# Second layers one turn later, odd tiles through the DMA transpose, and a condition around the last two half slots

## The chip, the core and the metric

The kernel runs on one core of a Trainium2 chip. The metric is the device time of one execution in microseconds, lower is better. Times of several runs are given by their median.

## What is computed

Three stages, on x of shape (8, 3072, 256); after the first one the 24576 rows of 256 are tokens:

```python
# 1: a filter in the frequency domain along the sequence
X = np.fft.rfft(x, axis=1)
y = np.fft.irfft(X * F[None], n=3072, axis=1)
# 2: a layer of 1024, then back to 256
h = y @ w_in
e = np.exp(h - h.max(-1)); sm = e / (e.sum(-1) + 1e-9)
solu = h * sm
ln = (solu - mu) / np.sqrt(var + 1e-6) * g_ln
x2 = ln @ w_out
# 3: one of 8 experts for each token, by the largest cosine
logits = normed(x2) @ normed(expert_emb).T / tau
idx = logits.argmax(1); gate_w = softmax(logits)[row, idx]
out[idx == e] = gate_w * (np.maximum(x2 @ w1[e], 0) @ w2[e])
```

## The kernel before

**Precision.** Every large matmul is made of three f16 matmuls (high x high, high x low, low x high), which is why tiles are split into a high and a low half by one ACT copy and one DVE subtraction.

**Stage B** (`stage_b`) goes over 192 tiles of 128 tokens, 48 for each of four pairs of batches. Turn i of its loop issues, in program order: the transposes of tile i-1 (`turn`) if it has any; the exponential of tile i on ACT (L929) and its product on DVE (L930), which make `es`; in even turns the inverse transform of two more tiles (`inv4`, L710 to L716); the second layer of tile j = i - LAG (L945, 24 matmuls into `o`); work from other generators (`aux`); the first layer of tile i+1 (`begin`, `mm1`, L728, 12 matmuls of 512 columns into the PSUM tile `h`) and its row maximum (`top`, L893). Engines keep program order, so the order of these calls is the order on every queue. `h` has two buffers; a tile that is turned keeps its buffer until T is out, as its transposes are written into it.

The second layer needs `es` transposed, as f16 halves, in `T`. There are two ways to it. `turn` (L899) makes eight f32 transposes on PE into `h`, an ACT copy (L907) and a DVE subtraction (L908). `send` (L910) makes the ACT copy (L914) and the subtraction (L915) first, from `es` into `hl`, and one DMA from SP's queue (L917) transposes the result into `T`. In the first three pairs even tiles are turned at the start of the next turn and odd tiles are sent at the end of their own turn, behind the second layer; in the last pair every tile is turned.

`aux` gives out side work: in pairs 0 to 2 the Fourier transforms of the next pair (`fft`) and the maxima of the expert weights (`w_max`); in the last pair, from turn LAG of it, the split of the expert weights into `wexp` (`w_split`, L452 and L460), done by turn SPLIT. Every eight second layers a group is closed by `b_final`, which runs over the next turns, chooses experts and places, and scatters the tokens' numbers into lists. `early` (`first_slots`), one step per turn at the end, makes the first table of slots.

**Stage C** (`stage_c`) goes over 110 slots: 89 of 256 tokens, then 21 half slots of 128. A slot is one expert's block of tokens: `load_slot` gathers the rows (POOL, L1121) and transposes them by DMA (SP, L1126), `weights` copies the expert's weights (DVE, L1149), then comes the first layer (L1197), its split (L1200, L1201), the second layer (L1160, for half slots one slot later), a scaling on ACT (L1163) and a scatter into the output on POOL (`scatter`, L164). The tables (`table`, `other_slots`) say which expert and tokens a slot has; 21 half slots are the most that any routing can need, and a slot that is not needed gathers an empty row and its scatter writes nothing. `run` opens the pools: `bx` for the tiles of pairs 0 to 2, `bp` for those of the last.

Of the kernel before, what the change touches and what calls it, by code (L numbers as in the profile page):

```python
# [32 lines left out]
EARLY = 24  # L33
LAG = 2
FIRST = 2
UNITS = 24 + 8 + 64 + 4
READY = 42
SPLIT = 38
WAIT = 4
MAGIC = 0x5F3759DF  # L40

# [111 lines left out]
class Build:  # L153
# [703 lines left out]
    def stage_b(self, xp, bps, gp, ps, hp, op, aux, early):  # L857
# [63 lines left out]
        for i in range(n + LAG):  # L921
            j = i - LAG
            now = 0 <= i < n
            if 0 <= i - 1 < n and i != n - 1 and (i % 2 or i > n - N2):
                turn(i - 1)
            if now:
# [22 lines left out]
            if now:  # L949
                if i % 2 and i < n - N2:  # L950
                    send(i)
                aux(*divmod(i, N2), 0)
                if i + 1 < n:
                    begin(i + 1)
                    top(i + 1)
                jk = L["pool"].tile([128, FF], BF16, name="jk", tag="jk")
                nc.scalar.activation(jk, L["s"], AF.Square, accum_out=col(i, "st", 2))
# [8 lines left out]
            if 0 <= j < n:  # L966
# [13 lines left out]
                if k == G - 1:  # L980
                    p, nn = divmod(j - (G - 1), N2)
                    finals.append((self.b_final(groups.pop(j // G), p, nn, gp, ps, j // G == n // G - 4, j // G < n // G - 4), 0))
            if i >= n - N2 + SPLIT + 2:
                next(early, 0)
# [23 lines left out]
    def table(self, sp, tp, ps, nb, start, K, blk, out):  # L1008
# [19 lines left out]
        v.scalar_tensor_tensor(taken, taken, 0.0, nb, op0=ALU.max, op1=ALU.min)  # L1028
        out["taken"] = taken
        yield  # L1030
        ge = sp.tile([128, E], F32, name="ge", tag="ge")
# [63 lines left out]
    def other_slots(self, sp, tp, ps):  # L1095
# [15 lines left out]
        yield  # L1111
        yield from self.table(sp, tp, ps, nb, x2, rest, 128, {})

# [15 lines left out]
    def stage_c(self, cb, hp, op, ps, side):  # L1129

        nc = self.nc
        wt = {}

        def load(s):
            while s >= len(self.tables):
                if next(side, 1) == 1:
                    return
            for _ in self.load_slot(s, cb):
                pass
# [12 lines left out]
        def second(M):  # L1152

            tab, k, w2, hh, hl, fs = M
            for h in range(tab["nh"]):
# [10 lines left out]
                next(side, 0)  # L1166

        weights(0, 0)
        next(side)
        load(1)  # L1170
        weights(0, 1)
        s = 0
        late = None
        while s in self.loaded:
            load(s + 2)
            xT = self.loaded.pop(s)
            tab, k = self.tables[s]
            w1, w2 = wt[s]
            n = tab["nh"] * 128
            w1 = w1.rearrange("p (l k f) -> p l k f", l=2, k=2)  # L1180
            w2 = w2.rearrange("p (l k f) -> p l k f", l=2, k=8)
            m = 512 // n
            fs = 1024 // n
            hh, hl = [], []
            for j in range(8 // m):
                if j == 8 // m - 2:
                    weights(s + 1, 0)
                if m * j % fs == 0:
                    hh.append(cb.tile([128, fs, n], F16, name="chh", tag="chh", bufs=2))
                    hl.append(cb.tile([128, fs, n], F16, name="chl", tag="chl", bufs=2))  # L1190
                t = (ps.tile([128, m, n], F32, name="a", tag="a") if j % 2 else hp.tile([128, m, n], F32, name="h", tag="h"))
                for i in range(m):
                    f = m * j + i
                    q = 0
                    for db in range(2):
                        for l, r in ((0, 0), (1, 0), (0, 2)):
                            nc.tensor.matmul(t[:, i, :], w1[:, l, db, f * 128:(f + 1) * 128], xT[:, r + db, :n], start=q == 0, stop=q == 5)  # L1197
                            q += 1
                sl = slice(m * j % fs, m * j % fs + m)
                nc.scalar.activation(hh[-1][:, sl, :], t, AF.Relu)  # L1200
                nc.vector.scalar_tensor_tensor(hl[-1][:, sl, :], t, 0.0, hh[-1][:, sl, :], op0=ALU.max, op1=ALU.subtract)  # L1201
                next(side, 0)
            if late:
                second(late)
            weights(s + 1, 1)
            late = (tab, k, w2, hh, hl, fs)
            if tab["nh"] > 1:
                second(late)
                late = None
            wt.pop(s)  # L1210
            s += 1
        if late:
            second(late)


    def run(self):
        tc, nc = self.tc, self.nc
        last = self.np_run - 1
        with (
# [14 lines left out]
            bps = [None, None]  # L1234
            bps[0] = right.enter_context(Tags(tc, "bx", {"nm": 2, "es": 2, "jk": 1, "hl": 2, "T": 3}, side="right"))
            ap = right.enter_context(tc.tile_pool(name="ap", bufs=2, side="right"))
            with (
# [3 lines left out]
                with tc.tile_pool(name="pp", bufs=1) as pp:  # L1241
# [5 lines left out]
                    for pool, tag in ((xp, "c4"), (xp, "xh"), (gp, "rows")):  # L1247
                        self.m1 += [pool.tile([128, 4, 128], F32, name=tag, tag=tag, bufs=2) for _ in range(2)]
                    self.m1 += [pp.tile([128, 4, 128], F32, name=f"m1_{k}") for k in range(2)]
                    for _ in self.fft(0, ap, ps, hp):  # L1250
# [14 lines left out]
                def last_pool():  # L1265
                    for _ in ffts:
                        pass
                    mid.close()
                    bps[1] = mid.enter_context(Tags(tc, "bp", {"nm": 2, "es": 2, "jk": 1, "T": 3}))

# [83 lines left out]
```

## Time and profile before

| | before |
|---|---|
| median of 3 runs | 2769.92 us (2764.28 to 2777.8) |
| the profiled execution | 2770.33 us |
| its span, first to last instruction | 2768.5 us |
| mean granted clock of TensorE | 0.983 |
| PE, DVE, ACT, POOL busy | 2642.6, 1897.8, 1529.8, 1245.2 us |

The span is what the profile covers; the execution's own time lies 1.8 us above it. Times in rows are microseconds from the span's start. PE is TensorE's matmuls, PEld its weight loads, DVE VectorE, ACT ScalarE, POOL GpSimd, SP SyncE; a q behind a name is that engine's sequencer. Busy times are unions, so two overlapping instructions count once. The releaser of a wait, behind an arrow, is inferred from semaphores.

### The profile page before, as it was taken

To read this page: it belongs to the slowest core of one execution; us is meant where nothing else is said; L and a number is where in the kernel's file an instruction comes from. 1 tells how busy PE (TensorE), PEld (TensorE's weight loads), DVE (VectorE), ACT (ScalarE), POOL (GpSimd) and SP (SyncE) were. 2 spreads that over 40 slices of the span, in tenths; PEclk is the share of its full clock that TensorE was granted. 3 is DMA by queue.
4 is the path that set the end of the run, shared out by engine and by line. 5 is a ranking of instruction groups with operands and counts; after the bars stand their busy time and mean duration, and the time that the engine had idled before them with its cause. 6 is when DMAs were issued, how large, how long until landed. Compare 5 with 4: busy or idle time off the path is not lost.

```text
span 2768.5 us, 53941 instructions
## 1 busy us (share of the span) xinstructions
PE 2642.6 (95%) x20234; PEld 2035.6 (74%) x20234; DVE 1897.8 (69%) x2976; ACT 1529.8 (55%) x2858; POOL 1245.2 (45%) x2633
## 2 busy tenths in 40 slices
PE   6889999999999998999999998999999999999998
PEld 5447666666666675666677777888888888888898
DVE  5846888867898768988788985554544545545465
ACT  3556777767777766877788864323333333333332
POOL 2001245434555444554455556744454444544444
PEclk8999999999999999999999999999999999999999
DMA  9868888799787798876444432332222333223222
GB/s 316 221 178 248 196 209 185 186 218 211 178 196 181 204 231 201 187 172 140 104 123 121 120 72 50 78 77 73 77 77 75 78 75 78 76 75 79 75 59 57
DMA packets 445398, 384.66 MB, mean 139 GB/s; under 512 B 285995, under 2 KB 368053, under 8 KB 442064
## 3 DMA queue, kind: packets, MB, share of 16 engines
q1 hardware_dynamic: 392288, 310.60, 46.6%
q0 software_dynamic: 27088, 57.48, 6.8%
q10 hardware_dynamic: 25760, 13.14, 1.8%
q8 instruction: 159, 2.61, 0.4%
q14 instruction: 103, 0.84, 0.1%
HBM read 195.93 MB, written 103.35 MB: 108 GB/s over the span
## 4 chain that ended last, share of the span: by engine, by line
PE 30%; issue 23%; POOL 19%; DVE 14%; DMA 8%; ACT 4%; SPq 1%; POOLq 0%; ACTq 0%; DVEq 0%
PE h L728 10%; PE o L945 9%; POOL crow L1121 7%; POOL out_dram L164 6%; POOL scr L163 3%; DVE nm L893 3%; DVE es L930 2%; PE a L512 2%; PE h L904 2%; PE a L667 2%; PE a L710 2%; DMA bufA<-out 2%; DMA c<-bufC 1%; DVE T L908 1%; ACT hl L914 1%
## 5 line engine op out<-in xcount | busy, mean ns | idle before, releaser
L945 PE MATMUL o<-wo_h,T 128*128 128x264 f16 x3072 | 552.8, 277 | 3.3 <-DMA T<-hl 3.2
L1160 PE MATMUL o<-cw,chh 128*128 128x256 f16 x3184 | 527.6, 273 | 0.0
L728 PE MATMUL h<-win_h,xh 128*128 128x512 f16 x1536 | 497.3, 385 | 25.8 <-DVE T L908 22.5
L1197 PEld LDWEIGHTS <-cw 128*128 128x128 f16 x5280 | 476.1, 98 | 57.3 <-POOL gu L761 6.5
L945 PEld LDWEIGHTS <-T 128*128 128x128 f16 x4608 | 452.4, 98 | 70.0 <-DMA T<-hl 3.6
L896 POOL TENSOR_SCALAR gcc<-nm 128x1 f32<-128x1 f32 x192 | 118.6, 618 | 813.3 <-DVE nm L894 533.6
L728 PEld LDWEIGHTS <-xh 128*128 128x128 f16 x2304 | 223.6, 99 | 310.3 <-issue 81.2
L1160 PE MATMUL o<-cw,chl 128*128 128x256 f16 x1592 | 434.0, 273 | 3.0 <-DVE chl L1201 3.0
L945 PE MATMUL o<-wo_l,T 128*128 128x264 f16 x1536 | 425.5, 277 | 0.0
L164 POOL DMA_INDIRECT out_dram<-cot,ids x199 | 218.4, 1097 | 454.8 <-ACT cot L1163 443.0
L1201 DVE SCALAR_TENSOR_TENSOR chl<-h,chh 128x512 f16<-128x512 f32 x199 | 135.8, 683 | 392.1 <-ACT chh L1200 392.1
L1160 PEld LDWEIGHTS <-chh 128*128 128x128 f16 x3184 | 310.6, 98 | 35.5
L1163 ACT ACTIVATE cot<-o,fac 128x256 f32<-128x256 f32 x199 | 94.5, 475 | 423.8 <-PE o L1160 421.8
L1149 DVE COPY cw<-wexp 128x4096 f16 x220 | 279.9, 1280 | 44.3 <-PE o L1160 23.6
L893 DVE TENSOR_REDUCE nm<-h 128x1 f32<-128x1024 f32 x192 | 234.0, 1219 | 105.5 <-PE h L728 105.3
L1197 PE MATMUL h<-cxT,cw 128*128 128x256 f16 (+1 forms) x2640 | 295.1, 263 | 6.8 <-POOL gu L761 6.2
L728 PE MATMUL h<-win_l,xh 128*128 128x512 f16 x768 | 295.9, 385 | 0.0
L1197 PE MATMUL a<-cxT,cw 128*128 128x256 f16 (+1 forms) x2640 | 294.0, 262 | 0.0
L930 DVE SCALAR_TENSOR_TENSOR es<-h,gcc,es 128x1024 f32<-128x1024 f32 x192 | 245.6, 1279 | 65.3 <-ACT es L929 49.4
L929 ACT ACTIVATE es<-h,nm,isc_h 128x1024 f32<-128x1024 f32 x192 | 230.7, 1201 | 61.6 <-DVE nm L894 46.0
L1121 POOL DMA_INDIRECT crow<-xs,ids x199 | 203.5, 1022 | 65.8 <-issue 63.8
L164 POOL DMA_INDIRECT lst<-gdi,gix x192 | 209.1, 1089 | 35.1 <-issue 32.9
(262 smaller groups left out, 4355.9 us busy)
## 6 DMA issues: line engine op xcount, KB each, us to landing
wst<-in_w_dram SPq DMA_DIRECT2D x128, 256.0 KB
in<-in_x_dram SPq DMA_DIRECT2D x48, 512.0 KB
in<-bufA SPq DMA_DIRECT2D x64, 384.0 KB
c<-bufC SPq DMA_DIRECT2D x96, 256.0 KB
xs<-rows SPq DMA_DIRECT2D x96, 256.0 KB
ft<-in_filt_dram SPq DMA_DIRECT2D x24, 960.0 KB
bufA<-out SPq DMA_DIRECT2D x72, 256.0 KB
zw<-z SPq DMA_DIRECT2D x96, 192.0 KB
```

Of the source, the lines that this page charges most:

```text
L164: ins = self.nc.gpsimd.indirect_dma_start(in_offset=None, **kw).ins
L728: nc.tensor.matmul(h[:, nb, :], l[:, i, db, :], r[:, db, sl], start=k == 0, stop=k == 5)
L893: nc.vector.tensor_reduce(x[:, 0:1], L["h"], axis=AX.X, op=ALU.max, negate=True)
L896: nc.gpsimd.tensor_scalar(cc, nm, nm, 1.0, op0=ALU.mult, op1=ALU.max)
L929: nc.scalar.activation(L["s"], L["h"], AF.Exp, bias=L["nm"], scale=self.isc_h[:, i // N2:i // N2 + 1], accum_out=col(i, "st", 0))
L930: nc.vector.scalar_tensor_tensor(L["s"], L["h"], col(i, "cc", 0), L["s"], op0=ALU.mult, op1=ALU.mult, accum_out=col(i, "st", 1))
L945: nc.tensor.matmul(o[:, :D + E], T[:, l, :], r[:, f, :], start=q == 0, stop=q == 23)
L1121: nc.gpsimd.indirect_dma_start(out=rows[:, h, :], out_offset=None, in_=self.xs, in_offset=bass.IndirectOffsetOnAxis(ap=tab["ids"][:, h, k: ...
L1149: nc.vector.tensor_copy(w.rearrange("p (o k) -> p o k", o=1), self.wexp[:, bass.ds(e, 1), part * 4096:(part + 1) * 4096])
L1160: nc.tensor.matmul(o[:, :D], l[f // fs][:, f % fs, h * 128:(h + 1) * 128], w2[:, r, f, :], start=q == 0, stop=q == 23)
L1197: nc.tensor.matmul(t[:, i, :], w1[:, l, db, f * 128:(f + 1) * 128], xT[:, r + db, :n], start=q == 0, stop=q == 5)
L1201: nc.vector.scalar_tensor_tensor(hl[-1][:, sl, :], t, 0.0, hh[-1][:, sl, :], op0=ALU.max, op1=ALU.subtract)
```

## The change

LAG is 3 in place of 2, so the second layer of tile j stands in turn j + 3. Odd tiles are sent at the start of the turn after their own, where even tiles are turned, in all four pairs; tile 191 is still turned. `T` has four buffers, and the last pair's pool has one `hl`. The split of the expert weights and `early` start one turn later. Two of the first matrices move from the pool `pp` to tiles `mt` of `ap`. In stage C the table keeps the count of half slots that hold tokens (`used`); the loop over slots becomes a function, stops two slots early, and runs the last two only if the count is over 19.

```diff
-LAG = 2
+LAG = 3
+SPARE = 2
...
-            if 0 <= i - 1 < n and i != n - 1 and (i % 2 or i > n - N2):
-                turn(i - 1)
+            if 0 <= i - 1 < n and i != n - 1:
+                (turn if i % 2 or i == n else send)(i - 1)
...
             if now:
-                if i % 2 and i < n - N2:
-                    send(i)
                 aux(*divmod(i, N2), 0)
...
-            if i >= n - N2 + SPLIT + 2:
+            if i >= n - N2 + SPLIT + LAG:
                 next(early, 0)
...
         out["taken"] = taken
+        used = out["used"] = tp.tile([1, 1], I32, name=f"used{len(self.tables)}")
+        v.tensor_copy(used, src[0:1, E - 1:E])
...
-        yield from self.table(sp, tp, ps, nb, x2, rest, 128, {})
+        t2 = {}
+        yield from self.table(sp, tp, ps, nb, x2, rest, 128, t2)
+        self.used = t2["used"]
...
+        stop = [None]
         def load(s):
...
+            if stop[0] is not None and s >= stop[0]:
+                return
...
+        def slots(s):
+            late = None
+            while s in self.loaded:
...
+        n = self.np_run * 2 * S
+        full = -(-(n - E * (BLK - 1)) // BLK)
+        rest = (n - full * BLK - E) // 128 + E
+        end = full + rest
+        stop[0] = end - SPARE
         weights(0, 0)
         next(side)
         load(1)
         weights(0, 1)
...
+        slots(0)
+        assert len(self.tables) == end
+        used = nc.values_load(self.used[0:1, 0:1], min_val=0, max_val=end)
+        with tc.If(used > rest - SPARE):
+            stop[0] = end
+            for s in range(end - SPARE, end):
+                load(s)
+            weights(end - SPARE, 0)
+            weights(end - SPARE, 1)
+            slots(end - SPARE)
...
-            bps[0] = right.enter_context(Tags(tc, "bx", {"nm": 2, "es": 2, "jk": 1, "hl": 2, "T": 3}, side="right"))
+            bps[0] = right.enter_context(Tags(tc, "bx", {"nm": 2, "es": 2, "jk": 1, "hl": 2, "T": 4}, side="right"))
...
-                    self.m1 += [pp.tile([128, 4, 128], F32, name=f"m1_{k}") for k in range(2)]
+                    self.m1 += [ap.tile([128, 4, 128], F32, name="mt", tag="mt", bufs=3) for _ in range(2)]
...
-                    bps[1] = mid.enter_context(Tags(tc, "bp", {"nm": 2, "es": 2, "jk": 1, "T": 3}))
+                    bps[1] = mid.enter_context(Tags(tc, "bp", {"nm": 2, "es": 2, "jk": 1, "hl": 1, "T": 4}))
```

## Rows read from the trace of the kernel before

**Rows 1.** Page, part 1: busy us, share of span, instructions.

```profile
PE 2642.6 (95%) x20234; PEld 2035.6 (74%) x20234; DVE 1897.8 (69%) x2976; ACT 1529.8 (55%) x2858; POOL 1245.2 (45%) x2633
```

**Rows 2.** Windows by stage: start:end length, PE, PEld, DVE, ACT, POOL busy, clock, DMA share, GB/s.

```profile
186.00:596.90 410.90, 386.78 (x2406) 262.25 (x2405) 319.02 (x506) 294.68 (x554) 143.94 (x400) 0.98 0.82 200
...
1366.10:1704.00 337.90, 322.58 (x2387) 236.68 (x2386) 281.62 (x544) 252.59 (x485) 183.37 (x539) 0.99 0.39 100
1704.00:2760.50 1056.50, 1049.04 (x10081) 942.99 (x10081) 544.47 (x689) 332.37 (x598) 531.23 (x663) 1.00 0.29 74
```

**Rows 3.** Windows again: a full stretch, eight turns of pair three, eight of the last.

```profile
750.00:800.00 50.00, 48.70 (x322) 32.94 (x320) 47.39 (x78) 41.05 (x77) 29.97 (x66) 1.00 0.78 179
1314.90:1366.10 51.20, 50.26 (x356) 35.23 (x355) 40.35 (x83) 38.27 (x75) 25.21 (x83) 1.00 0.48 103
1474.00:1528.60 54.60, 53.35 (x395) 39.20 (x394) 48.34 (x89) 44.38 (x85) 29.14 (x84) 1.00 0.46 120
```

**Rows 4.** Waits of PE: us, times, longest; 186 to 1366.1, last row 1366.1 to 1700.

```profile
PE h L728 <- DVE T L908: 17.1, 11, 3.7
PE a L710 <- DMA c<-bufC: 6.7, 4, 3.0
...
PE o L945 <- DMA T<-hl: 3.2, 2, 2.8
...
PE h L728 <- DVE T L908: 5.4, 5, 1.3
```

**Rows 5.** Timeline of PE, one even turn of the last pair: start, length, instruction.

```profile
1482.68 0.38 PE L728 MATMUL h<-win_h,xh 128*128 128x512 f16 x1
...
1485.27 1.04 PE L904 MATMUL h<-cst,es 128*128 128x128 f32 x8
1486.14 1.06 PE L710 MATMUL a<-mt,c 128*128 128x128 f32 x8
1489.73 0.38 PE L728 MATMUL h<-win_h,xh 128*128 128x512 f16 x1
```

**Rows 6.** Groups by line, whole span: busy us, mean ns, idle before, releasers.

```profile
L908 DVE TENSOR_TENSOR T<-h,T 128x1024 f16<-128x1024 f32 x120 | 145.1, 1209 | 30.2 <-ACT T L907 29.9
...
L915 DVE TENSOR_TENSOR hl<-es,hl 128x1024 f16<-128x1024 f32 x72 | 88.1, 1223 | 43.3 <-ACT hl L914 43.3
```

**Rows 7.** Timeline of DVE in the same turns; idle before it in brackets.

```profile
1481.41 1.22 DVE L908 TENSOR_TENSOR T<-h,T 128x1024 f16<-128x1024 f32 x1
...
1485.47 1.23 DVE L893 TENSOR_REDUCE nm<-h 128x1 f32<-128x1024 f32 x1 [0.58 <-PE h L728]
```

**Rows 8.** DMA of 1900 to 2600: queue's packets, MB, share; issues.

```profile
q1 hardware_dynamic: 72199, 17.41, 13.2%
...
cxT<-crow SPq DMA_TRANSPOSE x133
```

**Rows 9.** Timeline of DVE in pair three, tiles 127 and 128.

```profile
1245.70 1.22 DVE L915 TENSOR_TENSOR hl<-es,hl 128x1024 f16<-128x1024 f32 x1 [0.73 <-ACT hl L914]
...
1247.97 1.21 DVE L893 TENSOR_REDUCE nm<-h 128x1 f32<-128x1024 f32 x1
```

**Rows 10.** Waits of SP's queue, 200 to 1366: us, times, longest.

```profile
SPq L917 <- DVE hl L915: 329.7, 59, 9.9
```

**Rows 11.** Timeline of PE: the first slot of stage C.

```profile
1703.95 2.72 PE L1197 MATMUL h<-cxT,cw 128*128 128x256 f16 x12 [6.23 <-POOL gu L761]
```

**Rows 12.** Timeline of PE and POOL at the end.

```profile
2745.35 1.50 PE L1197 MATMUL h<-cxT,cw 128*128 128x128 f16 x24 [0.20 <-DMA cxT<-crow]
...
2750.64 1.50 PE L1197 MATMUL h<-cxT,cw 128*128 128x128 f16 x24
...
2759.57 0.98 POOL L164 DMA_INDIRECT out_dram<-cot,ids  x1 [1.61 <-ACT cot L1163]
```

**Rows 13.** DMA of 2756.8 to the end: all packets.

```profile
DMA packets 96, 0.00 MB, mean 0 GB/s; under 512 B 96, under 2 KB 96, under 8 KB 96
```

**Rows 14.** Line 1147, DVE's sequencer: ns min/median/max, first and last start.

```profile
L1147 DVEq TENSOR_LOAD <-er x220: 299/307/707, 1698.7 to 2748.9; - x110
```

More of the change, by code (lines that the diff above doesn't have):

```diff
@@ L1129, in stage_c @@
     def stage_c(self, cb, hp, op, ps, side):
-        nc = self.nc
+        tc, nc = self.tc, self.nc
         wt = {}
+        stop = [None]
         def load(s):
@@ L1166, in second @@
                 next(side, 0)
+        def slots(s):
+            late = None
+            while s in self.loaded:
+                load(s + 2)
+                xT = self.loaded.pop(s)
+                tab, k = self.tables[s]
+                w1, w2 = wt[s]
+                n = tab["nh"] * 128
+                w1 = w1.rearrange("p (l k f) -> p l k f", l=2, k=2)
+                w2 = w2.rearrange("p (l k f) -> p l k f", l=2, k=8)
+                m = 512 // n
+                fs = 1024 // n
+                hh, hl = [], []
+                for j in range(8 // m):
+                    if j == 8 // m - 2:
+                        weights(s + 1, 0)
+                    if m * j % fs == 0:
+                        hh.append(cb.tile([128, fs, n], F16, name="chh", tag="chh", bufs=2))
+                        hl.append(cb.tile([128, fs, n], F16, name="chl", tag="chl", bufs=2))
+                    t = (ps.tile([128, m, n], F32, name="a", tag="a") if j % 2 else hp.tile([128, m, n], F32, name="h", tag="h"))
+                    for i in range(m):
+                        f = m * j + i
+                        q = 0
+                        for db in range(2):
+                            for l, r in ((0, 0), (1, 0), (0, 2)):
+                                nc.tensor.matmul(t[:, i, :], w1[:, l, db, f * 128:(f + 1) * 128], xT[:, r + db, :n], start=q == 0, stop=q == 5)
+                                q += 1
+                    sl = slice(m * j % fs, m * j % fs + m)
+                    nc.scalar.activation(hh[-1][:, sl, :], t, AF.Relu)
+                    nc.vector.scalar_tensor_tensor(hl[-1][:, sl, :], t, 0.0, hh[-1][:, sl, :], op0=ALU.max, op1=ALU.subtract)
+                    next(side, 0)
+                if late:
+                    second(late)
+                weights(s + 1, 1)
+                late = (tab, k, w2, hh, hl, fs)
+                if tab["nh"] > 1:
+                    second(late)
+                    late = None
+                wt.pop(s)
+                s += 1
+            if late:
+                second(late)
+        n = self.np_run * 2 * S
[3 more added lines that the diff above has]
+        stop[0] = end - SPARE
         weights(0, 0)
@@ L1171, in stage_c @@
         weights(0, 1)
[L1172 to L1213, printed above, removed]
+        slots(0)
[8 more added lines that the diff above has]
+            slots(end - SPARE)
     def run(self):
```

## The prediction

> **What bounds the kernel now.** I read the page first: PE is busy for 95% of the span, DVE for 69%, ACT for 55% [rows 1]. That average hides stages with different limits, so the next view is the windows by stage [rows 2]. Stage C (from 1704 us) has PE busy for 1049.04 of 1056.50 us with DVE at about half: it is bound by PE alone, and only less PE work makes it shorter. The last batch pair of stage B (1366.1 to 1704) has PE busy for 322.58 of 337.90 us, but DVE for 281.62 too. The first pair (186 to 596.9, the other two look alike) has PE busy for 386.78 of 410.90 us.
>
> Then I read three stretches of eight turns or 50 us [rows 3]. In the last pair eight turns take 54.60 us (1474.00 to 1528.60, from one exponential to the eighth after it), PE idle for 1.25 us of it. Eight turns at the end of the third pair, where odd tiles go by DMA and little Fourier work is left, take 51.20 us. The stretch 750 to 800 shows how near its limit DVE may run while PE still does 48.70 of 50 us: 47.39 us, 95%.
>
> The waits of PE come next [rows 4]: in the three first pairs, the longest sum is 17.1 us in which the first layer waits for the split of an evacuated transpose (DVE, L908), while PE waited for a T that came by DMA for 3.2 us in all. In the last pair the wait for L908 is 5.4 us. So hardly any time is lost because second layers come too early: a longer lag by itself has little to win.
>
> **The change, part by part.**
>
> *Odd tiles of the last pair sent by DMA.* A turn of an even index in the last pair is, on PE, first layer, eight transposes, the inverse transform, second layer, and the next first layer. The rows show it: first layer from 1482.68, transposes from 1485.27, inverse transform from 1486.14, next first layer from 1489.73 [rows 5]. The transposes hold PE for 1486.14 - 1485.27 = 0.87 us, and they stand in line with everything else: nothing hides them. The new rule sends tiles 145, 147, ... 189 (23 of them; tile 191 is still turned on PE, since i equals n there). 23 x 0.87 = 20.0 us of PE work leave a stage that is 95% PE. Per group of eight turns that is 4 x 0.87 = 3.5 us, 54.6 to 51.1, and the stretch of the third pair, which has this form already, took 51.2 [rows 3].
>
> What comes in for it: ACT and DVE do the same amount of work, for the split of the hidden tile (DVE 1223 ns) replaces the split of the transpose (1209 ns) [rows 6]. DVE's 48.34 us per group [rows 3] must then fit in 51.1 us, 94.6%, the share of the stretch 750 to 800. In an ordinary turn DVE still stands idle before the row maximum until PE has finished (0.58 us before the one at 1485.47) [rows 7], two such pauses per two turns, more than the 0.87 us that is taken away, so it does not become the bound in those; in turns that also carry a group's final steps it can. The other limit is a tie: the split of the even tile's transpose begins at 1481.41 and lasts 1.22 us, and the first layer that reuses its PSUM begins at 1482.68 [rows 5, 7]. Any DVE delay there costs PE. I take 18 of the 20.0 us, between 9 (half is lost to such delays) and 23 (the 1.25 us idle of some groups goes too).
>
> The transfers: a transpose by DMA in stage C, a quarter of T in bytes (128 x 512 against 128 x 2048 of f16), took 13.2% of 700 us / 133 = 0.69 us of all 16 engines [rows 8], so a T is about 2.8 us (an estimate from that row) and 23 of them 64 us, which take the DMA share of the last pair from 0.39 to about 0.58 [rows 2]. That stays under the 0.82 of the first pair, where the same transfers run. On SP's queue each of them waits for the DVE split; behind it stand the loads of the expert weights and of the inverse transform and the writes of xs, which are issued one to two turns before their use. I cost this at nothing; if that cover is too short, PE waits for bufC as in the first pairs (6.7 us in 4 times) [rows 4].
>
> *Odd tiles sent one turn later, in the first three pairs.* 72 tiles. Today the split sits in the odd turn behind the second layer: ACT's copy waits for the es of its own tile, and DVE's split (1245.70, 1.22 us) ends just before the Fourier step that precedes the row maximum of the following even tile (1247.97) [rows 9]. Afterwards it stands at the head of the even turn, ahead of that tile's exponential and es. The even tile's maximum can start up to 1.2 us earlier, its es gets 1.2 us of DVE work ahead of it: a swap, in the same chain. SP's queue, which waited 329.7 us in 59 times for this split [rows 10], comes to it after the loads of the turn instead of before them, so loads leave sooner. Against it, DVE's even turns become the heavier ones. Bounds: -14 us (most of the 17.1 + 3.2 us of rows 4 goes) and +14 us (the same waits nearly double). I take a gain of 4.
>
> *Lag of three turns.* The order on PE shifts the second layers by one turn, and no work is added. At the start of stage B one turn has no second layer; the rows of one turn put a second layer at some 2.5 us: 7.05 from one first layer to the next (1482.68 to 1489.73), less 2.59 of first layer, 0.87 of transposes and at most 1.06 of inverse transform [rows 5]. Other aux work stands in those turns, so it costs from 0 to 2.7 us (2.5 and a little latency), and I take 0.5, near nothing. At the end, the gather of the first slot is tied to the second layer of tile 189, behind which today stand one turn's transposes and two second layers, afterwards only the latter: PE's idle of 6.23 us before the first slot [rows 11] grows by up to 0.9, which I take. Together +1.4 (0 to +3.6).
>
> *The last two half slots.* In stage C's end a half slot is one first layer and one second layer: from 2745.35 to 2750.64, 5.29 us, all PE [rows 12]. Whether the body is skipped can be read: after the last two scatters were issued (from 2756.8), the DMA moved 96 packets of 0.00 MB [rows 13], so the last two slots held no row to write, and the table counts 19 or fewer. The body is not run. PE's last second layer then follows at 2745.35 instead of some 10.6 us later, and the last scatter moves up with it: -10.6.
>
> The condition adds on every engine a load of the count into a register, a compare and a jump over the body. DVE does such a load 220 times, 0.30 us each [rows 14]: that is the low end, with 0.2 for the arithmetic about 0.5 us. For the jump the trace has no row. The upper end is the longest stretch in which every engine waits for the program's end, from the end of the last scatter's issue (2759.57 + 0.98) [rows 12] to the span's end at 2768.5: 8.0 us, which it would cost if the condition forced one more such meeting. I take 4 us, the middle, as neither end is nearer. Net -6.6 (-10.1 to -2.6). The three small copies of the count on DVE lie beside other work and cost nothing.
>
> [...]
>
> **Sum.** -18 - 4 + 1.4 - 6.6 = -27.2. The profiled execution took 2770.33 us (span 2768.5), 0.4 above the median 2769.92, so the same sum serves both: 2743. The bounds of the four terms lie 5, 10, 1.4 and 3.5 us below and 9, 18, 2.2 and 4 us above; they don't all fall together, and the roots of the sums of their squares are 12 and 21 us: 2731 to 2764.
>
> **Rivals.**
> 1. *The condition eats what it skips.* It acts as a meeting of all engines, 8.0 us as at the program's end [rows 12], and the jump costs the other 2.6: nothing is left of the 10.6. For it: no row shows a jump, and the end of the program is paid after it. Against it: SP, ACT and DVE reach it early. 2743 + 6.6 = 2750. [...]
> 2. *DVE becomes the bound of the last pair.* For it: 94.6% of the time needed and the tie at 1482.68. Against it: the stretch 750 to 800. If half the turns lose 1 us, some 12 us of the 18 are gone: 2755.
> 3. *The even turn is overloaded in the first pairs (slower).* The send now puts 1.22 us of DVE work into the even turn, which also has the es of the even tile, the split of xh and the next tile's row maximum; if DVE has not worked these off when the even tile's transposes come at the start of the odd turn, their split (L908) and so the first layer two tiles on are late. It decides from the point where DVE has no pause in an even turn. If half of the 72 even tiles lose 1.22 us, +44 in the place of -4: 2791. Against it: the same 1.22 us leaves the odd turn just before, ahead of the same maximum.
> 4. *The waits of the first pairs vanish,* as the turns are better balanced: of the 17.1 + 6.7 + 3.2 us [rows 4] two thirds, 18, in place of the 4 taken, the other terms as they are: 2729.
> 5. *The body runs after all* (count over 19): the condition is paid and the slots too: 2743 + 10.6 = 2754. Rows 13 speak against it.
>
> **How the numbers follow.** The forecast, 2743, gets 0.61; rival 1 0.14, rival 2 0.12, rival 3 0.06, rival 4 0.05, rival 5 0.02. The range 2730 to 2764 holds the forecast with nearly all of its bounds, and rivals 1, 2 and 5. About 0.5% (13.8 us, the border at 2756) is what a measurement of this kernel can tell from no change. Faster: the forecast nearly whole, rivals 1 and 4, half of 2: 0.81. Same: 0.13. Slower: 0.06.
>
> **What would show it.** Right: 184 transposes fewer at L904 and 23 more T by DMA; groups of eight turns in the last pair at 51 to 52 us with DVE near 48 us of busy time; the three first pairs within 14 us of the 1180 us that they took together; the last matmul about 10.6 us sooner measured from the start of stage C, and from the last scatter to the span's end some 4 us more than 8. Wrong: groups still at 54 us with PE waiting for L908 in most odd turns (rival 2); waits of the first layer for L908 well over 17 us in the first pairs (rival 3); over 15 us from the last scatter to the end (rival 1); ten more half-slot groups at the end (rival 5).

## The result: 1.1% slower, and the profile after

The changed kernel takes 2804.98 us against 2773.86 us of the kernel before on the same chip: ratio 1.0109, 95% interval 1.0079 to 1.0138. 2743 was forecast. Its profiled execution has a span of 2804.3 us (before 2768.5). Its lines in stage B are those of before plus one; "+1" is not said again below. In the other kernels lines move a little further, so go by the names of the tiles there: `c` is the input of the inverse transform, `wst` the expert weights as loaded, `ft` the filter of the Fourier transforms.

I cut each trace at the first exponential of tiles 0, 48, 96 and 144 (pairs 0 to 2 and the last), at the first matmul of stage C and at the last scatter. Lengths in us, for the two kernels and for all runs told of below. The same code differs in these sums by up to 12 us from one profiled execution to another (pairs 0 to 2 of after and of `e_turned`), so small differences in the table decide nothing by themselves; the ratios are of many executions.

| kernel | pair 0 | pair 1 | pair 2 | sum 0 to 2 | last pair to slot 0 | to last scatter | to end | median | ratio to before, 95% |
|---|---|---|---|---|---|---|---|---|---|
| before | 410.9 | 388.7 | 380.5 | 1180.1 | 337.9 | 1055.6 | 9.0 | 2773.86 | 1 |
| after | 397.1 | 406.5 | 403.2 | 1206.8 | 351.8 | 1047.1 | 10.8 | 2804.98 | 1.0109 (1.0079 to 1.0138) |
| e_cond | 403.9 | 394.1 | 381.6 | 1179.6 | 337.0 | 1044.5 | 10.8 | 2759.90 | 0.9959 (0.9942 to 0.9976) |
| e_lag | 407.8 | 394.7 | 384.8 | 1187.3 | 340.7 | 1058.2 | 9.0 | 2777.68 | 1.0030 (1.0015 to 1.0045) |
| e_turned | 395.0 | 408.8 | 391.5 | 1195.3 | 340.1 | 1047.0 | 10.8 | 2780.16 | 1.0030 (1.0011 to 1.0048) |
| e_issue0 | 391.7 | 399.5 | 385.0 | 1176.2 | 335.1 | 1046.7 | 10.8 | 2758.08 | 0.9963 (0.9947 to 0.9978) |
| e_issue | 393.1 | 389.4 | 379.3 | 1161.8 | 334.9 | 1044.4 | 10.8 | 2737.96 | 0.9882 (0.9849 to 0.9916) |
| e_actq | 392.2 | 391.6 | 377.6 | 1161.4 | 335.5 | 1047.0 | 10.8 | 2739.27 | 0.9884 (0.9851 to 0.9916) |
| e_head | 396.6 | 406.3 | 390.1 | 1193.0 | 338.8 | 1045.3 | 10.8 | 2779.63 | 1.0044 (1.0032 to 1.0056) |
| e_own | 407.1 | 392.0 | 381.1 | 1180.2 | 350.8 | 1046.8 | 10.8 | 2781.10 | 1.0034 (1.0016 to 1.0052) |
| e_own2 | 403.1 | 390.0 | 381.7 | 1174.8 | 344.8 | 1046.1 | 10.8 | 2764.88 | 0.9988 (0.9970 to 1.0006) |
| e_issue_t | 391.7 | 390.5 | 375.8 | 1158.0 | 339.9 | 1046.5 | 10.8 | 2747.12 | 0.9929 (0.9912 to 0.9945) |
| e_even | 392.5 | 386.3 | 378.0 | 1156.8 | 363.5 | 1044.6 | 10.8 | 2770.20 | 1.0008 (0.9996 to 1.0020) |
| e_evenq | 392.2 | 392.5 | 377.6 | 1162.3 | 331.1 | 1044.7 | 10.8 | 2737.68 | 0.9888 (0.9860 to 0.9915) |

So pair 0 became shorter, pairs 1 and 2 lost 18 and 23 us, the last pair lost 14 where 18 were to be won, and stage C won what was forecast (8.5 us up to the last scatter, less 1.8 behind it). The windows by stage of after (columns as in [rows 2]), from the start of pair 0, 1, 2, the last pair and stage C:

```profile
187.90:585.00 397.10, 379.26 (x2390) 258.97 (x2389) 316.97 (x502) 293.77 (x552) 159.49 (x395) 0.99 0.86 210
585.00:991.40 406.40, 379.29 (x2418) 259.38 (x2416) 325.31 (x536) 288.25 (x549) 205.46 (x495) 0.97 0.81 191
991.40:1394.70 403.30, 372.51 (x2385) 253.40 (x2383) 319.99 (x540) 283.04 (x539) 207.47 (x496) 0.96 0.71 161
1394.70:1746.50 351.80, 316.51 (x2232) 221.23 (x2230) 284.65 (x548) 254.21 (x488) 201.22 (x546) 0.98 0.62 130
1746.50:2804.30 1057.80, 1041.18 (x9937) 934.56 (x9937) 537.21 (x683) 328.76 (x592) 525.67 (x657) 0.99 0.29 74
```

Pairs 1 and 2 in the same view of before:

```profile
596.90:985.60 388.70, 372.92 (x2420) 254.91 (x2419) 322.99 (x534) 287.61 (x550) 183.86 (x493) 1.00 0.83 200
985.60:1366.10 380.50, 368.55 (x2395) 249.75 (x2394) 319.40 (x542) 281.95 (x537) 187.84 (x498) 0.99 0.74 172
```

Of the 40.5 us that pairs 1 and 2 lost, 10.3 are PE's busy time (379.29 - 372.92 + 372.51 - 368.55) at a lower granted clock, 0.97 and 0.96 in the place of 1.00 and 0.99; the other 30.2 are new idle time. Its cause stands in the waits of PE (us in total, times, longest) in pairs 0 to 2 of after, to be held against [rows 4]:

```profile
PE a L711 <- DMA c<-bufC: 39.2, 10, 6.3
...
PE h L729 <- DVE T L909: 7.4, 6, 2.7
```

The wait that the change was to shorten did shorten, from 17.1 to 7.4 us. But the inverse transform now waits 39.2 us for the load of its input from bufC, where it waited 6.7. SP's timeline at the longest of these waits (start, duration of the issue; all are in the one queue of SP), and PE's row after it:

```profile
1166.76 0.33 SPq L556 DMA_DIRECT2D ft<-in_filt_dram  x1
1167.14 0.42 SPq L419 DMA_DIRECT2D wst<-in_w_dram  x1
1167.65 6.66 SPq L918 DMA_TRANSPOSE T<-hl  x1
1174.36 0.58 SPq L698 DMA_DIRECT2D mt<-in_m_dram  x1
1174.99 0.41 SPq L700 DMA_DIRECT2D c<-bufC  x1
...
1181.00 2.05 PE L711 MATMUL a<-mt,c 128*128 128x128 f32 x8 [6.26 <-DMA c<-bufC]
```

The same place in before:

```profile
1156.49 0.33 SPq L555 DMA_DIRECT2D ft<-in_filt_dram  x1
1156.87 0.42 SPq L418 DMA_DIRECT2D wst<-in_w_dram  x1
1157.35 0.42 SPq L697 DMA_DIRECT2D mt<-in_m_dram  x1
1157.81 0.87 SPq L699 DMA_DIRECT2D c<-bufC  x1
...
1164.93 1.05 PE L710 MATMUL a<-mt,c 128*128 128x128 f32 x8
...
1165.20 1.74 SPq L917 DMA_TRANSPOSE T<-hl  x1
```

In before the load leaves right behind the filter load, and its transform starts at 1164.93, 7.1 us later, without a wait; the send comes after both. In after the send stands at the head of the even turn, ahead of that turn's two loads in the program: SP spends 6.66 us on issuing the transpose, and only then are the loads issued. PE gets its data 6.0 us after the issue (1174.99 to 1181.00), near the median of such loads in `e_actq` (5.4 us, below). Without its wait of 6.26 us PE would have started the transform 8.0 us behind the issue of the filter load, as it does in before (8.4): the wait is about as long as the transpose's issue.

Nine of the waits for bufC in pairs 0 to 2 are longer than 0.5 us, and at each of them the filter load stands one or two issues ahead of the transpose, whose issue then takes 4.65 to 6.66 us. At six of the nine SP had first waited 8.4 to 10.7 us with that load (by its releaser, until DVE was done with an earlier filter), and then took up the transpose within 0.5 us of the issue ahead, so the split was ready there. These waits of SP, in pairs 0 to 2 of after and of before:

```profile
SPq L556 <- DVE zw L591: 87.8, 11, 10.7
...
SPq L555 <- DVE zw L590: 49.9, 11, 7.1
```

So the transposes cost most where the queue is late already. These late loads alone do no harm: `e_issue`, below, has 82.5 us of them in 11 times.

After PE's idle time at 1181 the eight matmuls take 2.05 us instead of 1.05. The windows of after there show the granted clock fall and come back, 0.94, then 0.63, then 1.00; taken by single microseconds, it is 0.50 in each from 1181 to 1185, 0.81 in the next and 1.00 from 1186 to 1188:

```profile
1160.00:1181.00 21.00, 13.79 (x88) 8.20 (x86) 18.59 (x35) 13.65 (x27) 13.32 (x25) 0.94 0.66 133
1181.00:1187.00 6.00, 6.00 (x33) 4.94 (x34) 3.15 (x6) 1.99 (x3) 1.70 (x8) 0.63 1.08 274
1187.00:1192.00 5.00, 5.00 (x27) 2.74 (x26) 2.19 (x4) 2.58 (x6) 0.13 (x1) 1.00 0.41 120
```

In the last pair the same queue holds up the expert weights, which ACT splits at L461. There the issue of a transpose is short, 1.3 to 3.9 us with a median of 1.9; what is long is SP's wait for DVE's split at the head of the turn, with the expert weights' loads behind it. SP's waits of that kind, one of them in SP's timeline, and ACT's waits:

```profile
SPq L918 <- DVE hl L916: 102.5, 23, 9.4
...
1499.19 0.46 SPq L439 DMA_DIRECT2D wst<-in_w_dram  x1
1505.64 1.98 SPq L918 DMA_TRANSPOSE T<-hl  x1
...
1509.14 0.90 SPq L439 DMA_DIRECT2D wst<-in_w_dram  x2
...
ACT wexp L461 <- DMA wst<-in_w_dram: 38.9, 16, 6.9
```

ACT's wait was 2.3 us in 3 times in before. ACT's order puts the hidden tile's copy and the next exponential behind that step, so es comes late and with it the transposes and the split for which the first layer waits: PE waits for L909 13.9 us in 16 times (before 5.4 in 5 [rows 4]).

In stage C, no first layer runs beyond slot 107, and the last row of POOL is:

```profile
2793.54 0.98 POOL L165 DMA_INDIRECT out_dram<-cot,ids  x1 [1.61 <-ACT cot L1170]
```

From there to the span's end it takes 10.8 us, before 9.0 [rows 12].

### The profile page after: what moved, and what is told of

The parts are those of the page before. It is cut to its first block, busy times and chain, and to the rows that moved or that the text cites. A ratio compares the mean times of both kernels' runs of the same rounds, so it can differ in the third digit from the quotient of the medians.

```text
span 2804.3 us, 53387 instructions
## 1 busy us (share of the span) xinstructions
PE 2634.5 (94%) x19906; PEld 2016.1 (72%) x19906; DVE 1893.9 (68%) x2971; ACT 1528.8 (55%) x2852; POOL 1315.0 (47%) x2627
## 4 chain that ended last, share of the span: by engine, by line
PE 35%; issue 22%; POOL 18%; DVE 11%; DMA 9%; ACT 2%; SPq 2%; POOLq 0%; ACTq 0%; DVEq 0%
PE h L729 12%; PE o L946 10%; POOL crow L1124 7%; POOL out_dram L165 6%; POOL scr L164 3%; PE a L668 3%; PE a L513 2%; DMA c<-bufC 2%; DVE nm L894 2%; PE a L711 2%; PE h L905 2%; DMA wst<-in_w_dram 1%; POOL gcc L897 1%; DMA zw<-z 1%; DMA bufA<-out 1%
## 5 line engine op out<-in xcount | busy, mean ns | idle before, releaser
L946 PE MATMUL o<-wo_h,T 128*128 128x264 f16 x3072 | 562.5, 280 | 4.8 <-DVE rows L973 4.2
L897 POOL TENSOR_SCALAR gcc<-nm 128x1 f32<-128x1 f32 x192 | 158.8, 827 | 796.3 <-DVE nm L895 560.6
L165 POOL DMA_INDIRECT lst<-gdi,gix x192 | 233.5, 1216 | 35.8 <-issue 33.1
```

Of the source, the lines that this page charges most:

```text
L165: ins = self.nc.gpsimd.indirect_dma_start(in_offset=None, **kw).ins
L897: nc.gpsimd.tensor_scalar(cc, nm, nm, 1.0, op0=ALU.mult, op1=ALU.max)
L946: nc.tensor.matmul(o[:, :D + E], T[:, l, :], r[:, f, :], start=q == 0, stop=q == 23)
```

## The experiments

Theory A: the order of SP's queue costs the time. The transposes by DMA now stand ahead of the loads of their turn, and these come late. Rival B: the split's new place on ACT and DVE, ahead of the even tile's exponential and product, costs it. Rival C: the lag of three itself. Beside them stands the question what the condition costs.

**The condition alone** (`e_cond`): after with stage B as in before.

```
-LAG = 3
+LAG = 2
-                (turn if i % 2 or i == n else send)(i - 1)
+            if 0 <= i - 1 < n and i != n - 1 and (i % 2 or i > n - N2):
+                turn(i - 1)
...
+                if i % 2 and i < n - N2:
+                    send(i)
```

> Stage B as before, stage C with the condition and without the last two half slots. The traces of before and after show the way from the first slot's first matmul to the last scatter shorter by 8.6 us and the way from there to the span's end longer by 1.8. Theory A (the loss lies in stage B, in the order of SP's queue): about 7 us less than before, 2764 to 2769. If the price of the condition is the 4 us of the prediction's sum or the 8 of its upper bound: 2767 to 2771. If the condition takes part in the loss (code that is fetched anew, another order of the slots): 2774 or more.

Measured: 0.9959, 11 us less (7 to 16); its median of 2759.90 lies some 4 us below the range that theory A gave. Its last scatter starts 1044.5 us after stage C's first matmul, 11.1 us sooner than before, and 10.8 us ahead of the end, 1.8 later. The condition costs about 1.8 us behind the last scatter and leaves 9.3; it has no part in the loss.

**The lag alone** (`e_lag`): before with `LAG = 3` and four T buffers.

```
-LAG = 2
+LAG = 3
-"hl": 2, "T": 3}
+"hl": 2, "T": 4}
```

> Before with second layers three turns behind and a fourth T buffer, the sends where they were, the last pair turned on PE, all slots run. Theory A (the place of the send in SP's queue costs the time): within 8 us of before, 2766 to 2782. Rival C (the lag itself: transposes, second layers and final steps fall together otherwise): it carries most of the loss of pairs 1 and 2, some 40 us, so 2795 to 2815.

Measured: 1.0030, 8 us more (4 to 12). Rival C in the size that it needs has fallen. Small and real costs stay: PE's waits for bufC rise to 15.6 us in 6 times in pairs 0 to 2, and the way from tile 191's exponential to slot 0 takes 20.4 us in the place of 16.2.

**No sends in the last pair** (`e_turned`): after with one condition changed.

```
-                (turn if i % 2 or i == n else send)(i - 1)
+                (turn if i % 2 or i > n - N2 else send)(i - 1)
```

> After with all tiles of the last pair turned on PE, as in before. Pairs 0 to 2 are those of after (28.6 us later at the start of the last pair). If the sends of the last pair cost what they save (theory A: ACT waits 38.9 us for expert weights that queue behind them), the last pair takes its 338 us again and the whole is some 7 us under after: 2793 to 2800. If the sends of the last pair did save their 20 us and lag or something else took them back: 2815 to 2825.

Measured: 1.0030; the expected range was missed at its lower side, because pairs 0 to 2 came out 11 us shorter than in after, with the same code. The last pair takes 340.1 us, as with the lag alone, against 351.8 with sends: as after makes them, the sends of the last pair cost 12 us more than the transposes that they replace. By the ratios the two kernels are 22 us apart; why pairs 0 to 2 differ in the same code stays open.

**The DMA issued later** (`e_issue0`, `e_issue`). ACT's and DVE's part of the send stays at the head of the even turn. Only the issue of the transpose moves: in `e_issue0` behind the loads of the inverse transform and of the turn's first half, in `e_issue` behind the two loads of the inverse transform alone. `ship()` issues the transpose that `send` left in `out`; of its two places below the first is that of `e_issue`, the second that of `e_issue0`.

```
-            nc.sync.dma_start_transpose(out=T, in_=hl.rearrange("p a b -> p (a b)"))
+            out.append((T, hl))
...
                 xs.append(next(src, None))
+            ship()
...
                 aux(*divmod(i, N2), 0)
+                ship()
```

> After with one thing moved: ACT's and DVE's part of the send stays at the head of the even turn, but the DMA transpose is issued on SP behind the turn's loads of the inverse transform and of the first half's Fourier or expert-weight step. Theory A (what stands behind the send on SP comes late): PE's waits of 5 to 6 us for bufC in pairs 1 and 2 are gone, ACT's waits for expert weights shrink from 38.9 us to under 10, and the time falls to 2745 to 2772. Rival B (the split's place on ACT and DVE, ahead of the even tile's exponential and product, costs the time): nothing changes on those engines, 2795 to 2810.

> After with the DMA transpose issued right behind the two loads of the inverse transform, ahead of the Fourier and expert-weight loads of the turn. In the run with the issue behind those too, PE waited 32 us in 16 times in pairs 1 and 2 for a T that came late. If the inverse transform's loads are what came late in pairs 1 and 2: those waits stay away, the waits for T shrink below 16 us, pairs 1 and 2 take under 780 us together (784.5 there, 809.7 in after). If the expert weights are what came late in the last pair, its waits return: some 10 us more there than the 335 of that run. Together 2750 to 2770. If the Fourier loads count as well in pairs 1 and 2: 2775 to 2795.

Measured: 0.9963 and 0.9882. One line of the program moved past two loads makes 1.0109 into 0.9882, some 63 us (2.27% of 2769). Rival B has fallen: nothing moved on ACT and DVE. PE's waits for bufC in pairs 0 to 2 are down to 1.6 us in 4 times in `e_issue` and 1.4 in 3 in `e_issue0`. PE's longest waits there, first of `e_issue0`, then of `e_issue`:

```profile
PE o L953 <- DMA T<-hl: 32.1, 18, 3.7
```

```profile
PE o L954 <- DMA T<-hl: 13.8, 9, 2.2
```

Issued too late, T itself is missed by the second layer; behind just the two loads, more than half of that goes too. `e_issue` came out better than its range. In the last pair its expected return of the waits for expert weights did not come: ACT waits for them 9.6 us in 10 times, though they stand behind the transpose as in after. SP's rows in `e_issue` at the place shown above show the exchange itself; the transpose still takes 5.45 us to issue, but nothing urgent is behind it:

```profile
1133.02 0.33 SPq L556 DMA_DIRECT2D ft<-in_filt_dram  x1
1133.40 0.42 SPq L419 DMA_DIRECT2D wst<-in_w_dram  x1
1133.87 1.38 SPq L698 DMA_DIRECT2D mt<-in_m_dram  x1
1135.29 0.43 SPq L700 DMA_DIRECT2D c<-bufC  x1
1135.82 5.45 SPq L916 DMA_TRANSPOSE T<-hl  x1
```

**The loads taken off SP** (`e_actq`): after with the send untouched, the loads of the inverse transform and of the expert weights issued by ACT.

```
-            nc.sync.dma_start(mt, a["m4"][:, n:n + 2, :])
+            nc.scalar.dma_start(mt, a["m4"][:, n:n + 2, :])
```

(and likewise for the bufC load and the two expert-weight loads)

> After with the send where it is, at the head of the even turn with its DMA, but the loads of the inverse transform and of the expert weights issued by ACT instead of SP. Nothing of the send moves; what stood behind it on SP no longer does. Theory A by queue order: PE's waits for bufC and ACT's for expert weights go away as with the later issue, without the waits for a late T: 2740 to 2765 (ACT's issues cost some of it). If it is the transfer itself, the 512 KB of a transpose on the DMA engines ahead of the loads, that delays them: no change, 2790 to 2810.

Measured: 0.9884, as `e_issue`, at the lower end of its range. The transposes stand ahead of the loads in the program as in after, and the hardware queues take as much of the 16 DMA engines' time from 590 to 1360 us (69.4 + 8.7%, 76.1% in after), and they do no harm; so it is SP's queue and not the transfer on the engines. The loads take 5.4 us from issue to landing (DMA issues of 590 to 1360 us; the last number is that median):

```profile
c<-bufC ACTq DMA_DIRECT2D x48, 256.0 KB, 5.4
mt<-in_m_dram ACTq DMA_DIRECT2D x48, 128.0 KB, 3.5
...
T<-hl SPq DMA_TRANSPOSE x49, 6.7
```

**Without SP's wait for the split** (`e_head`): the split at the tile's own odd turn, the transpose at the head of the next turn. This was to part two readings of theory A.

```
+            ship()
-                (turn if i % 2 or i == n else send)(i - 1)
+            if 0 <= i - 1 < n and i != n - 1 and (i % 2 or i == n):
+                turn(i - 1)
...
+                if i % 2 and i < n - 1:
+                    send(i)
```

> ACT's and DVE's split back at the tile's own odd turn, the DMA transpose at the head of the next, even turn, ahead of its loads, as in after. SP's wait for the split is then short or nil, but the 512 KB transfer still stands ahead of the loads in SP's queue. If it is SP's wait that makes the loads late: they leave on time, PE's waits for bufC stay away, 2745 to 2765 (pair 0 with the split at its old place some 405 us, pairs 1 and 2 some 770 together). If it is the transfer's place ahead of them in the same queue: the waits are there as in after, 2785 to 2805.

Measured: 1.0044, between its two ranges; pairs 1 and 2 take 796.4 us (809.7 in after, 800.3 in `e_turned`, 768.7 in `e_issue`). For pairs 0 to 2 my first reading, that SP waits for DVE's split, has fallen: that wait shrank from 138.4 to 18.2 us there and PE's wait for bufC stayed. The three rows are SP's wait of after, SP's of `e_head` and PE's of `e_head`:

```profile
SPq L918 <- DVE hl L916: 138.4, 39, 6.6
...
SPq L916 <- DVE hl L923: 18.2, 23, 1.6
...
PE a L711 <- DMA c<-bufC: 33.1, 10, 6.2
```

What stays there is the issue of the transpose. At a wait of 4.93 us of PE in `e_head`:

```profile
826.68 0.32 SPq L556 DMA_DIRECT2D ft<-in_filt_dram  x1
827.06 6.49 SPq L916 DMA_TRANSPOSE T<-hl  x1
833.59 0.58 SPq L698 DMA_DIRECT2D mt<-in_m_dram  x1
834.22 0.42 SPq L700 DMA_DIRECT2D c<-bufC  x1
```

Over pairs 0 to 2 the 72 issues of T have a median near 1.9 us in before, 3.4 in after, 3.6 to 4.1 in `e_issue` and 3.8 to 4.8 in `e_head`; the shortest of these took 1.3 us, the longest 8.3. They are long where loads were issued just ahead of them, and in before SP mostly stood idle ahead of the send. That the loads ahead are the reason is read from these rows alone; no run varied it by itself.

In the last pair the first reading holds. `e_head` takes 338.8 us there against 351.8 in after; SP waits for the split 10.6 us in 7 times instead of 102.5 in 23, no wait of ACT for expert weights is longer than 0.3 us, and the issue of a transpose has become longer, not shorter (median 2.9 us, 1.9 in after). So in pairs 0 to 2 it is the issue, and in the last pair the wait ahead of it, that holds SP's queue.

**Sends of the last pair at their own turn** (`e_own` with lag three, `e_own2` with lag two, both with the condition).

```
-                (turn if i % 2 or i == n else send)(i - 1)
+            if 0 <= i - 1 < n and i != n - 1 and (i % 2 or i == n):
+                turn(i - 1)
...
+                if i % 2 and i < n - 1:
+                    send(i)
                 aux(*divmod(i, N2), 0)
```

> After with the whole send back at its own turn, as in before, but in the last pair too; lag of three and the condition stay. Theory A: pairs 0 to 2 as with the lag alone (408, 395, 385 us), the send of the odd turn stands behind that turn's loads of the inverse transform (which belong to even turns); in the last pair it stands ahead of the expert-weight loads of the odd turn only, so the pair gains part of the 20 us: 2745 to 2765. If any DMA send in the last pair costs what it saves (DVE or the DMA engines too full): 2765 to 2775.

> Before with the condition (11 us less) and the odd tiles of the last pair sent at their own turn, lag of two. If the prediction's 18 us for the transposes is there once the send stands in the old place: 2740 to 2748. If the lag of three is needed for it, because T is wanted two turns after a send that waits for DVE: 2752 to 2765, with waits of the second layer for T in the last pair.

Measured: 1.0034 and 0.9988; against `e_cond` (0.9959) the sends of the last pair make `e_own2` some 8 us slower. Neither went as expected. The second layer does not wait for T there; the first layer waits for the split of the even tile's transpose, in `e_own2`:

```profile
PE h L729 <- DVE T L909: 24.2, 16, 2.6
```

That does not show that the split must come a turn later: `e_head` has it at the same place as `e_own`, with only the issue a turn later, and its last pair takes 338.8 us, 350.8 in `e_own`. In `e_own` ACT again waits for expert weights, 21.7 us in 17 times. So there too it is the place of the issue on SP.

**What the sends of the last pair are worth** (`e_issue_t`): `e_issue` with the last pair turned on PE, by the edit of `e_turned`.

> The run with the issue right behind the inverse transform's loads, with the last pair turned on PE as in before. What the transposes by DMA in the last pair are worth by themselves, the loads being on time. The prediction's term: 18 us more than that run, 2754 to 2758. By the stages of the runs so far (the last pair and the way to the first slot took 334.9 us there, 340.7 with the lag alone): 6 us more, 2742 to 2746, because DVE binds the turns that lose their transposes.

Measured: 0.9929, 9 us more than `e_issue` by the medians, 13 by the ratios (their intervals, of four executions each, all but touch), 5.0 by the stage (339.9 and 334.9). The windows of the last pair, `e_issue_t` first:

```profile
1344.80:1684.70 339.90, 326.74 (x2416) 239.63 (x2414) 283.17 (x548) 252.95 (x488) 185.11 (x543) 1.00 0.36 99
...
1346.90:1681.80 334.90, 310.05 (x2231) 220.72 (x2229) 282.86 (x548) 256.58 (x488) 206.78 (x544) 0.99 0.62 137
```

PE has 16.7 us less to do, near the 20.0 of the forecast, but its idle time grows by 11.7: its waits for L909 go from 3.8 us in 10 times to 11.0 in 16, and 4.9 us for rows (L981) are new.

**DVE's order in the last pair** (`e_even`, `e_evenq`): in `e_issue` the expert-weight step of an even turn's second half is moved to the next turn; `e_evenq` also issues those loads a step earlier.

```
-                        advance("s", split[0], 70 * (u - 2 * LAG) / (2 * (SPLIT - LAG)))
+                        if n2 % 2 or not half:
+                            advance("s", split[0], 70 * (u - 2 * LAG) / (2 * (SPLIT - LAG)))
...
-            if u < 62:
-                load(u + 2)
+            if u < 61:
+                load(u + 3)
```

> The run with the issue right behind the inverse transform's loads, and in the last pair the expert-weight step of an even turn's second half moved to the next odd turn's first half (two steps there), so that DVE comes to the split of the even tile's transpose without that step's 0.74 us ahead of it. If DVE's order at this point takes back the gain of the last pair (PE waited 11.0 us in 16 times for that split): 5 to 10 us less, 2728 to 2734. If DVE is short of time over the whole turn, the wait moves to another operation: 2735 to 2742.

> The run that moved the expert-weight step to the odd turns, with each expert-weight load issued one step earlier (three ahead instead of two). There ACT waited 53.6 us in 16 times for these loads, since both steps of an odd turn wanted loads that stand behind the even turn's writes of rows on SP; the last pair took 293.2 us from its start to tile 184. With the loads earlier that wait should be under 15 us. If DVE's 0.74 us ahead of the split of the even tile's transpose is then what binds the last pair: from its start to tile 184 in 255 to 262 us (265.3 without the move), in all 2728 to 2735. If DVE is short over the whole turn, or the two steps together hold ACT up ahead of the odd tile's exponential: 263 to 275 us there, 2736 to 2750.

Measured: 1.0008 and 0.9888. `e_even` missed both of its ranges: the two steps of an odd turn come upon loads that stand behind the writes of rows on SP; ACT waits, es is late, and the transposes with it:

```profile
ACT wexp L461 <- DMA wst<-in_w_dram: 53.6, 16, 4.9
...
PE h L905 <- DVE es L938: 21.8, 14, 3.4
```

With the loads a step earlier both waits are gone, and PE's wait for the split falls from 11.0 us in 16 times (`e_issue`) to:

```profile
PE h L730 <- DVE T L910: 4.3, 12, 0.8
```

From the last pair's start to tile 184 it takes 261.4 us, 265.3 in `e_issue`. So the place of this step in DVE's order does bind there; but the whole is the same as `e_issue`, so 4 us of a stage are all that can be said. `e_issue`, `e_actq` and `e_evenq` beat both kernels by over 1%.

## Why the prediction was wrong, by its own steps

**The step that failed** is the cost of the transposes on SP's queue, in both parts of stage B: what stands behind one there was taken to lose nothing. For the last pair I wrote "I cost this at nothing; if that cover is too short, PE waits for bufC as in the first pairs (6.7 us in 4 times)". That step names the wait for the split and the loads behind it, and only its price was wrong: SP waited 102.5 us in 23 times, ACT 38.9 us for expert weights and PE 4.9 us for bufC, and the pair lost 13.9 us. For the first pairs I wrote that SP comes to the send "after the loads of the turn instead of before them, so loads leave sooner". That holds for the loads of the odd turn's two halves, which stood behind the send. The even turn's two loads of the inverse transform I did not place: in the diff the send moves ahead of the line that issues them, and they leave later. How little slack they had could be read: in pairs 1 and 2 of before the bufC load is issued a median of 10.4 us, and at the least 5.7, ahead of its first matmul (8.8 and 4.9 in after, 13.9 and 6.0 in `e_issue`). What takes it away, the duration of a transpose's issue on SP, I did not cost at all, though SP's timeline of before has a row for each, 1.74 us in the one above and up to 6.6. PE's waits for bufC came to 39.2 us. With only that order mended the sign of the forecast is right: `e_issue` has 0.9882, 33 us less, where 27 were forecast. That the sizes are near is luck: its last pair won less than its term and its first pairs over four times theirs, and the two made up for each other.

What the issue's duration stands for is read from the traces of this case: the transpose's 6.66 us kept the next load from being issued (1167.65 to 1174.36), the c load's 0.41 us was followed by 5.6 us until PE had its data, so that the 0.41 us are not the movement of the data, and `e_head`, with 18.2 us of waits for the split where after has 138.4, kept most of the loss of pairs 1 and 2.

**Last pair, -18.** After: +13.9. In the good order 5 us are won by the stage and 9 to 13 by the runs (`e_issue` and `e_issue_t`). The first part of the step was right: PE's busy time fell by 16.7 us. The second was mis-sized: PE's idle time takes back 11.7, 7.2 of it as waits at the tie that I named. Rival 2, 12 of 18 lost, is near this in size; it had 0.12. DVE is not the bound of the whole stage, busy for 282.86 of 334.9 us in `e_issue`, and by `e_evenq` part of the loss is one step's place in its order.

**Sends a turn later, -4 (-14 to +14).** Both bounds were too narrow, and the sign hung on the queue. Against the lag alone pairs 0 to 2 went from 1187.3 to 1206.8 in after, and to 1161.8 in `e_issue`: +20 or -26. Rival 4 (the waits of the first pairs vanish, 18 us) is near what `e_issue` won against before, 18.3, but not in its mechanism: the three waits that it names are 22.1 us there and 27.0 in before, 13.8 of the 22.1 now for T. Of the 18.3 us, 17.8 stand in pair 0, and there 8.3 are PE's busy time, with 16 matmuls fewer and a granted clock of 0.99 for 0.98. What raised the clock is open; and pair 0 took 403.9 us in `e_cond` with stage B as in before, so part of the gain is scatter. Its window in `e_issue`, to be held against [rows 2]:

```profile
185.00:578.10 393.10, 378.49 (x2390) 259.26 (x2389) 316.85 (x502) 293.73 (x551) 161.27 (x391) 0.99 0.87 210
```

Rival 3 was right in the sign and near in size, not in its mechanism: the waits for L908 fell from 17.1 to 7.4 us.

**Lag, +1.4 (0 to 3.6).** Mis-sized: 8 us (4 to 12) alone, of which the junction to slot 0 shows 4.

**Tail, -6.6 (-10.1 to -2.6).** The mechanism was right; the price of the condition was mis-sized, 1.8 us behind the last scatter in the place of 4, and the gain is 9.3 by the stages, 11 by the ratio of `e_cond` (6.7 by the stages of after). The 0.2 us for the arithmetic in its lower bound stand in no row of before that is shown; in after it takes 0.19 us on SP (L1229). Rivals 1 and 5 did not come. For the jump, which had no row, after has one on each engine (L1230): the compare and jump takes 0.05 to 0.07 us on SP, DVE, ACT and POOL and 2.93 us on PE's queue, from 2791.9. How the 1.8 us come out of these is not shown.

**What stays open.** Why ACT's wait for expert weights fell from 38.9 to 9.6 us in `e_issue`, though they stand behind the transpose as in after, is settled in part: SP's wait for the split ahead of it fell from 102.5 us in 23 times to 59.5 in 22, and from the start of the transpose to the first of these loads it is 2.1 us, 3.6 in after (medians up to tile 184), since the two loads of the inverse transform no longer stand between. No run varied this by itself. Nor was it tried to set the length of a transpose's issue by what stands ahead of it.

## What to carry to other kernels

A DMA that is moved takes its issue time with it (6.66 us at the place shown): read the durations of the issues on the queue's own timeline, list what stands behind the new place in program order, and compare each one's slack with that time. It also takes its waits along: what it waits for at its new place holds up all that is behind it (102.5 us of SP's waits in the last pair of after, 38.9 us of ACT's behind them). When a planned gain turns into a loss and the engines' order looks right, move only the issue, or send the loads from another queue: both single edits here turned +1.1% into -1.2%. And of work taken from an engine that is 95% busy, count as gain only what the next engine in line leaves room for (5.0 of 16.7 us in the last pair here).

## What was not expected of the hardware

The issue of one 512 KB transpose by DMA kept SP in pairs 0 to 2 for 1.3 to 6.6 us in before, with a median of 1.9, where SP mostly stood idle ahead of it [rows 10], and for 1.3 to 7.9 us in after, with a median of 3.4, at the head of the even turn. The wait of PE of 6.26 us at 1181 in after cost more than itself: the granted clock of the following 6 us was 0.63, and eight matmuls of 1.05 us took 2.05. A condition over the last two slots, with a body that is skipped, cost 1.8 us behind the last scatter.
